# Causal attention on one core: the weights of three query blocks turned by VectorE and carried through DRAM

## The chip, the cores and the metric

The program runs on one core of one Trainium2 chip. A core has five engines that work side by side and wait for each other by semaphores: TensorE (PE in the rows; its weight loads, which overlap its products, are PEld), VectorE (DVE), ScalarE (ACT), GpSimd (POOL) and SyncE (SP), which here issues nearly all DMAs. TensorE writes into PSUM, and VectorE or ScalarE must move a result from there to SBUF before TensorE can read it. The metric is the device time of one execution in microseconds (us); lower is better.

## The reference

Three layers in a row. The first is banded attention (8 heads), the second a channel mix with three large products. The third, the one that the change touches, is causal attention by four experts with a gate that keeps two of them per token:

```python
# x: 4 batches, 576 tokens, 512 features; E = 4 experts, Hd = 64
logits = x @ w_gate                      # the 2 best experts of a token, softmax over their logits
for e in range(E):
    q, k, v = x @ wq[e], x @ wk[e], x @ wv[e]
    scores = q @ k.transpose(0, 2, 1) / 8
    scores = np.where(np.triu(np.ones((S, S)), 1), -1e9, scores)   # causal
    a = softmax(scores)                  # (…, 576, 576), zero above the diagonal
    out += gate_weight(e) * (a @ v @ wo[e])
```

The weights `a` come out with queries on the partitions and keys along the row. The product with `v` sums over keys, and TensorE sums over partitions, so each 128x128 block of `a` on or below the diagonal has to be turned first.

## The kernel before

Everything is float32; most products run as three products of a high and a low part (F32R), the turning and `a @ v` as plain float32.

The first two layers fill the program up to about 391 us. Neither their code nor the order of their instructions changes. Then comes the third layer, batch by batch (b = 0 to 3) and expert by expert (e = 0 to 3). The 576 tokens are cut into five blocks `TB`: one of 64 and four of 128. Its steps are generators:

- `queries_keys(b, g)` makes queries and keys for the expert pair g (experts 2g and 2g+1): 48 products of 288 columns (`pq`, `pk`, L394), a split into high and low parts, and 12 DMAs on SP (L681) that lay the parts out as `qs`, `kk` and `kl2`.
- `values(b)` makes `v` and the gate: 60 products of 260 columns (`pv`, L694).
- `scores(b, e)`: per query block t two products per piece of the row (`sc`, L768 and L770), a masked minimum on DVE into the row buffer `pe` (L774), the exponential with its row sum on ACT (L780); when all five blocks are there, three small DVE steps (L784 to L787), and then the scaling of the weights by 1/sum and gate, blocks 0 to 3 on DVE (L795) and block 4 on ACT (L793).
- `context(b, e)`: the 15 blocks are turned on PE as a product with `ident` (L815), four per PSUM tile, and copied to SBUF by ACT (L820) and DVE (L822) as `wt`. After the odd expert of a pair the products with `v` follow, key block by key block, for both experts at once on the two halves of TensorE's columns: widths of 512, 64, 512, 384, 256 and 128 columns (`av`, L841 and L846). Each float32 product leaves two records in the trace. Two copies give `ctx`.
- `project(b)`: 30 products of 512 columns with `wo` (`po`, L868) and 5 stores.

Which steps run beside which is set by a table `plan`: for each (b, e) it lists the generators and how many pieces of each `merge` takes in turn. From the program that results, a scheduler makes the order on each engine with cost estimates of its own; on the chip each engine then works its list off in that order. The same holds for SP: a DMA whose source is not ready holds up all DMAs behind it.

The buffers that matter: two row buffers `pe`, ten `wt` tiles, and PSUM tiles for scores (2), turned blocks (2), the `av` sum (1) and the other products (3).

Of the kernel before, what the change touches and what calls it, by code (L numbers as in the profile page):

```python
# [16 lines left out]
NEG = -8.0e9  # L17
# [4 lines left out]
def tile_dilated_attention__rwkv_channel_mix__moe_attention(  # L22
# [31 lines left out]
    xpool = ctx.enter_context(tc.tile_pool(name="xpool", bufs=1, side="left"))  # L54
    psum = dict(zip(("sc", "pt", "av", "mm"), [2, 2, 1, 3]))
    psum["pool"] = ctx.enter_context(tc.tile_pool(name="psum", bufs=2, space=bass.MemoryType.PSUM))

# [8 lines left out]
    still = cpool.tile([128, 512], BF16, name="still")  # L66
# [11 lines left out]
    def band(name, base, p1=0, j1=0):  # L78


        m = cpool.tile([128, WK], F32, name=name)
# [413 lines left out]
    with tc.tile_pool(name="apool", bufs=2, side="left") as ap:  # L495
# [90 lines left out]
        run(ga)  # L586

# [4 lines left out]

    TB = [(0, 64), (64, 128), (192, 128), (320, 128), (448, 128)]
    NB = len(TB)
    PO = [0, 64, 256, 576, 1024, 1600]
    NC2 = 3 * E * HD + E

    with s2:
        w2p = s2.enter_context(tc.tile_pool(name="w2p", bufs=1, side="left", reuse_waits="tile"))
        ep1 = s2.enter_context(tc.tile_pool(name="ep1", bufs=2, side="left", reuse_waits="tile"))  # L600
        def split_y(b):
            y = X[b][:, :, 1 : S + 1]
            yh = ep1.tile([128, KT, S], F32R, tag="yh", name=f"yh_{b}", bufs=1)
            yl = ep1.tile([128, KT, S], F32R, tag="yl", name=f"yl_{b}", bufs=1)
            for kt in range(KT):
                nc.scalar.copy(yh[:, kt, :], y[:, kt, :])
                nc.gpsimd.tensor_sub(yl[:, kt, :], y[:, kt, :], yh[:, kt, :].bitcast(F32))  # L607
            return yh, yl
# [4 lines left out]
        cmask = w2p.tile([128, S], F32, name="cmask")  # L613
        nc.gpsimd.memset(cmask, 0.0)
        nc.gpsimd.affine_select(out=cmask, in_=cmask, pattern=[[-1, S]], base=448,
                                channel_multiplier=1, compare_op=ALU.is_ge, fill=NEG)
# [3 lines left out]
        ahead = split_y(0)  # L620
        rawo = [w2p.tile([128, DM], F32, name=f"w2oraw{g}") for g in range(2)]
# [9 lines left out]
        for g in range(2):  # L631
            nc.sync.dma_start(rawo[g], wo[2 * g : 2 * g + 2].rearrange("e d f -> (e d) f"))
# [4 lines left out]
        for g in range(2):  # L637
            nc.scalar.copy(woh[:, g, :], rawo[g])
            nc.vector.tensor_sub(wol[:, g, :], rawo[g], woh[:, g, :].bitcast(F32))
# [5 lines left out]
        def begin(b, parts):  # L645


            qs = [ep.tile([128, 2, S], F32R, tag=f"qs{g}", name=f"qs_{b}_{g}", bufs=1) for g in range(2)]
# [4 lines left out]
            done[b] = (qs, kk, kl2, vt, gt)  # L653
            ys[b] = parts

        def queries_keys(b, g):

            qs, kk, kl2, vt, gt = done[b]
            yh, yl = ys[b]
# [4 lines left out]
            for c in range(2):  # L664
                cs = slice(CH * c, CH * c + CH)
                pq = ps("mm", f"pq_{b}_{g}_{c}")[:, :CH]
                pk = ps("mm", f"pk_{b}_{g}_{c}")[:, :CH]
                product(pq, (w2h, w2l), (yh[:, :, cs], yl[:, :, cs]), range(KT),
                        slice(128 * g, 128 * g + 128))
                product(pk, (w2h, w2l), (yh[:, :, cs], yl[:, :, cs]), range(KT),  # L670
# [5 lines left out]
                if c == 1:  # L676
                    emitted.add(("k", b, g))
                    for dst, src in ((qs[g][0:64], qh), (kk[g][0:64], kh), (qs[g][64:128], ql), (kk[g][64:128], kh),
                                     (kl2[g][0:64], kl), (kl2[g][64:128], kl)):
                        for j in range(2):  # L680
                            nc.sync.dma_start(dst[:, j, :].bitcast(F32), src[64 * j : 64 * j + 64, :].bitcast(F32))  # L681
                yield

        def values(b):

            qs, kk, kl2, vt, gt = done[b]
            yh, yl = ys[b]
            lg = logits[b % 2]
            for t, (t0, tn) in enumerate(TB):
                p = ps("mm", f"pv_{b}_{t}")[:tn, :260]  # L690
# [34 lines left out]
        def place(kb, t):  # L725

            t0 = TB[t][0]
            if kb == 0:
                return (3, 256) if t == 0 else (0, t0 - 64)
            if kb == 1:  # L730
                return 1, t0 - 64
            if kb == 2:
                return 2, t0 - 192
            if kb == 3:
                return 3, t0 - 320
            return 2, 384

        groups = [[(0, t) for t in range(1, NB)], [(1, t) for t in range(1, NB)],
                  [(2, 2), (2, 3), (2, 4), (4, 4)], [(3, 3), (3, 4), (0, 0)]]
        regions = [[(64, 0, 512)], [(128, 0, 512)], [(128, 0, 512)], [(128, 0, 256), (64, 256, 320)]]  # L740

# [5 lines left out]
        done, ys = {}, {}  # L747
# [4 lines left out]
        def scores(b, e):  # L752

            qs, kk, kl2, vt, gt = done[b]
# [3 lines left out]
            pe = ep1.tile([128, PO[NB]], F32, tag="pe2", name=f"pe2_{nm}", bufs=2)  # L758
            st = stats[e % 2]
            for t, (t0, tn) in enumerate(TB):  # L760
                n = t0 + tn
                tn = 128
                parts = [(0, n)] if n <= 512 else [(64, n), (0, 64)]
                for i, (c0, c1) in enumerate(parts):
# [3 lines left out]
                    nc.tensor.matmul(sc, qs[g][:, e % 2, t0 : t0 + 128], kk[g][:, e % 2, c0:c1],  # L768
                                     start=True, stop=False)
                    nc.tensor.matmul(sc, qs[g][:, e % 2, t0 : t0 + 128], kl2[g][:, e % 2, c0:c1],  # L770
                                     start=False, stop=True)
                    m = cmask[:tn, 448:512] if t == 0 else cmask[:, S - n + c0 : S - n + c1]
# [26 lines left out]
        heads = {}  # L799

        def context(b, e):

            vt = done[b][3]
            pe = weights.pop((b, e))
            g = e // 2
            nm = f"{b}_{e}"
            heads[e % 2] = []
            moved = []
            for i, grp in enumerate(groups):
                pt = ps("pt", f"pt2_{nm}_{i}")  # L810
                for kb, t in grp:
                    k0, kn = TB[kb]
                    tn = 128
                    c0 = place(kb, t)[1]
                    nc.tensor.transpose(pt[:kn, c0 : c0 + tn], pe[:tn, PO[t] + k0 : PO[t] + k0 + kn], ident[:tn, :tn])  # L815
                wt = ep.tile([128, 512], F32, tag="wt", name=f"wt{i}_{nm}", bufs=10)
                heads[e % 2].append(wt)
                for rows, c0, c1 in regions[i]:
                    if ("aava", "avav")[e % 2][i] == "a":
                        moved.append(nc.scalar.copy(wt[:rows, c0:c1], pt[:rows, c0:c1]))  # L820
                    else:
                        moved.append(nc.vector.tensor_copy(wt[:rows, c0:c1], pt[:rows, c0:c1]))  # L822
                yield
            if e % 2 == 0:
                return
            av1 = ps("av", f"av1_{nm}")
            av0 = ps("pt", f"av0_{nm}")
            two = [(64 * x, heads[x], vt[:, :, 64 * (2 * g + x) : 64 * (2 * g + x) + 64]) for x in range(2)]

            def after_all(ins):  # L830

                if kb == 0:
                    for m in moved:
                        tc.add_manual_dep(ins.ins, m.ins.name, together, reason="both experts' products together")

            for kb in range(NB):
                k0, kn = TB[kb]
                i, c0 = place(kb, max(kb, 1))
                q0 = max(k0, 64)
                for p0, w, vh in two:  # L840
                    ins = nc.tensor.matmul(av1[p0 : p0 + 64, q0 - 64 : 512], vh[:kn, kb, :], w[i][:kn, c0 : c0 + S - q0],  # L841
                                           start=(kb == 0), stop=(kb == NB - 1))
                    after_all(ins)
                if kb == 0:
# [13 lines left out]
        def project(b):  # L858

            for t, (t0, tn) in enumerate(TB):  # L860
# [9 lines left out]
                ob = ep.tile([128, DM], F32, tag="ob", name=f"ob_{b}_{t}", bufs=5)  # L870
# [7 lines left out]
        begin(0, ahead)  # L878
# [5 lines left out]
        def late(b):  # L884
            begin(b, split_y(b))
# [11 lines left out]
        plan = {(0, 0): [("c", 4), ("l1", 1), ("k0", 2), ("s", 6)],  # L897
# [55 lines left out]
```

## Time and profile before

| | us |
|---|---|
| median of three runs (597.89 to 602.9) | 601.97 |
| span of the profiled execution, first to last instruction | 600.2 |
| PE busy in the span | 568.9 |
| DVE busy | 334.7 |
| ACT busy | 369.2 |

A busy time is the time in which at least one instruction of the engine was under way. For the profiled execution only the span is known; it lies 1.8 us under the median of the runs and 2.3 us over the fastest of them. The third layer takes the last 209 us of the span.

### The profile page before, as it was taken

Reading aid. Unit: us, or ns where it says so; the run is one execution under the profiler, and the core shown is the slowest. Engines: PE = TensorE matmul, PEld = TensorE weight load, DVE = VectorE, ACT = ScalarE, POOL = GpSimd, SP = SyncE. Lnnn points to the kernel's source line nnn. Section 1 sums busy time; section 2 is a strip of 40 time slices with the busy share of each in tenths; the row PEclk is TensorE's granted clock in tenths of the full one; section 3 lists DMA queues with packets and bytes.
Section 4 is the critical chain, followed back from the end, with each engine's and each line's share of the span. In section 5 each row is a group of like instructions: output and inputs, shape, how many; then the busy total and the mean of one; then the engine's idle time right before and its main releaser. Section 6 shows DMA issues by size and latency. Waiting matters only on the chain.

```text
span 600.2 us, 12777 instructions
## 1 busy us (share of the span) xinstructions
PE 568.9 (95%) x4749; PEld 505.4 (84%) x4752; DVE 334.7 (56%) x1112; ACT 369.2 (62%) x1004; POOL 79.5 (13%) x101
## 2 busy tenths in 40 slices
PE   8987896999999999999999999999998999999986
PEld 4657796888999999999999999999986988987753
DVE  3567988854655355347254253527566556656552
ACT  3789957655698266597364742327656756755751
POOL 8300000000323012130003313003003003000000
PEclk9987889899999999999999999999999999999997
DMA  9990276638431321210000140043604514505302
GB/s 172 171 331 28 70 195 136 117 76 139 81 63 25 70 44 28 37 25 21 1 1 1 31 112 1 2 106 94 156 5 115 142 57 119 122 25 137 115 1 79
DMA packets 120461, 48.81 MB, mean 81 GB/s; under 512 B 104320, under 2 KB 108496, under 8 KB 120400
## 3 DMA queue, kind: packets, MB, share of 16 engines
q1 hardware_dynamic: 119984, 47.57, 34.4%
q8 instruction: 37, 0.61, 0.4%
q0 software_dynamic: 416, 0.44, 0.4%
q14 instruction: 24, 0.20, 0.1%
HBM read 29.11 MB, written 4.72 MB: 56 GB/s over the span
## 4 chain that ended last, share of the span: by engine, by line
PE 74%; ACT 13%; DVE 7%; issue 2%; DMA 2%; POOL 1%; SPq 0%; DVEq 0%; POOLq 0%; ACTq 0%
PE v L394 17%; PE h L394 13%; PE pv L694 5%; PE av L841 5%; PE pt L815 4%; PE po L868 4%; PE sc L267 4%; PE pk L394 4%; PE z L394 4%; PE pq L394 4%; PE av L304 3%; PE pt L294 2%; ACT pe L280 2%; PE sc L770 2%; PE sc L768 2%
## 5 line engine op out<-in xcount | busy, mean ns | idle before, releaser
L394 PE MATMUL h<-xh,wk_hi 128*128 128x288 f32 x256 | 80.2, 314 | 6.5 <-ACT r L407 4.2
L394 PE MATMUL h<-xl,wk_hi 128*128 128x288 f32 x256 | 77.8, 304 | 0.6 <-DVE xl L373 0.6
L394 PE MATMUL h<-xh,wk_lo 128*128 128x288 f32 x256 | 77.1, 301 | 0.0
L394 PE MATMUL v<-kh,wv_hi 128*128 128x288 f32 x256 | 76.2, 302 | 0.0
L394 PE MATMUL v<-kl,wv_hi 128*128 128x288 f32 x256 | 75.8, 299 | 0.0
L394 PE MATMUL v<-kh,wv_lo 128*128 128x288 f32 x256 | 75.0, 296 | 0.0
L394 PEld LDWEIGHTS h<-xh,wk_hi 128*128 128x128 f32 x256 | 49.5, 194 | 9.8 <-ACT r L407 5.3
L384 POOL TENSOR_TENSOR xl<-m,xh 128x1152 fp32r<-128x1152 f32 x12 | 32.1, 2674 | 168.5 <-ACT xh L383 148.9
L780 ACT ACTIVATE pe<-pe,st 128x64 f32<-128x64 f32 (+4 forms) x80 | 44.9, 563 | 15.3 <-DVE st L774 15.2
L394 PEld LDWEIGHTS h<-xl,wk_hi 128*128 128x128 f32 x256 | 49.5, 193 | 1.2 <-DVE xl L373 0.9
L394 PEld LDWEIGHTS h<-xh,wk_lo 128*128 128x128 f32 x256 | 49.6, 194 | 0.1
L394 PEld LDWEIGHTS v<-kh,wv_hi 128*128 128x128 f32 x256 | 47.8, 188 | 0.9 <-DVE r L408 0.2
L394 PEld LDWEIGHTS v<-kl,wv_hi 128*128 128x128 f32 x256 | 48.0, 188 | 0.5
L394 PEld LDWEIGHTS v<-kh,wv_lo 128*128 128x128 f32 x256 | 48.0, 188 | 0.2
L774 DVE CUSTOM_DVE_ANT_0 pe<-sc,cmask 128x64 f32<-128x64 f32 (+4 forms) x80 | 37.0, 475 | 19.5 <-PE sc L770 18.3
L280 ACT ACTIVATE pe<-pe,st 128x96 f32<-128x96 f32 x108 | 39.4, 368 | 13.2 <-DVE st L276 12.9
L407 ACT ACTIVATE r<-h 128x288 f32<-128x288 f32 x64 | 25.5, 409 | 30.4 <-PE h L394 21.6
L394 PE MATMUL z<-xh,wr_hi 128*128 128x288 f32 x128 | 39.9, 313 | 2.5 <-ACT z L401 2.5
L417 DVE TENSOR_TENSOR x<-v,z 128x288 f32<-128x288 f32 x32 | 14.5, 455 | 46.8 <-PE v L394 46.7
L370 DVE SCALAR_TENSOR_TENSOR m<-x,mus,m 128x288 f32<-128x288 f32 x64 | 30.0, 513 | 18.9 <-ACT m L369 18.7
L607 POOL TENSOR_TENSOR yl<-x,yh 128x576 fp32r<-128x576 f32 x16 | 20.8, 1332 | 138.4 <-DVE sm L713 46.4
L394 PE MATMUL z<-xh,wr_lo 128*128 128x288 f32 x128 | 39.1, 306 | 0.0
(169 smaller groups left out, 1522.4 us busy)
## 6 DMA issues: line engine op xcount, KB each, us to landing
kk<-kh SPq DMA_DIRECT2D x32, 144.0 KB, 2.6
kl<-kl SPq DMA_DIRECT2D x32, 144.0 KB, 2.6
raw_in_moe_w_k_dram<-in_moe_w_k_dram SPq DMA_DIRECT2D x4, 1024.0 KB, 9.5
raw_in_moe_w_v_dram<-in_moe_w_v_dram SPq DMA_DIRECT2D x4, 1024.0 KB, 5.7
out_dram<-ob SPq DMA_DIRECT2D x16, 256.0 KB, 2.5
rqk<-in_q_dram SPq DMA_DIRECT2D x48, 72.0 KB, 2.5
rqk<-in_k_dram SPq DMA_DIRECT2D x48, 72.0 KB, 2.5
vw<-in_v_dram SPq DMA_DIRECT2D x16, 192.0 KB, 3.5
```

The source lines that it names most:

```text
L267: nc.tensor.matmul(sc[h, c0 : c0 + WK], qT[h, QB * t : QB * t + QB], kT[h, k0 : k0 + WK], start=(b > 0), stop=(b > 0 or t == t1 - 1))
L280: nc.scalar.activation(pe[:, t, :], pe[:, t, :] if b else sc[:, c0 : c0 + WK], AF.Exp, bias=st[:, 0, t : t + 1], scale=-1.0, accum_out=st[ ...
L370: nc.vector.scalar_tensor_tensor(out=m, in0=x, scalar=mus[:, 0, w, f : f + 1], in1=m, op0=ALU.mult, op1=ALU.add)
L384: nc.gpsimd.tensor_sub(lo, m, hi.bitcast(F32))
L394: nc.tensor.matmul(o, w[:, kt, wsl], x[:, kt, :], start=(n == 0), stop=(n == last))
L407: nc.scalar.activation(r, p, AF.Relu)
L694: nc.tensor.matmul(p, x[:, kt, t0 : t0 + tn], w[:, kt, 512:772], start=(n == 0), stop=(n == 3 * KT - 1))
L774: nc.vector.tensor_tensor_reduce(out=pe[:tn, PO[t] + c0 : PO[t] + c1], in0=sc, in1=m, scale=-0.125, scalar=(BIG if i == 0 else st[:tn, 1, ...
L780: nc.scalar.activation(pb, pb, AF.Exp, bias=st[:tn, 0, t : t + 1], scale=-1.0, accum_out=st[:tn, 2, t : t + 1])
L815: nc.tensor.transpose(pt[:kn, c0 : c0 + tn], pe[:tn, PO[t] + k0 : PO[t] + k0 + kn], ident[:tn, :tn])
L841: ins = nc.tensor.matmul(av1[p0 : p0 + 64, q0 - 64 : 512], vh[:kn, kb, :], w[i][:kn, c0 : c0 + S - q0], start=(kb == 0), stop=(kb == NB - 1))
L868: nc.tensor.matmul(p, x[:, t0 : t0 + tn], w[:, g, :], start=(n == 0), stop=(n == 5))
```

## The change

It does five things, all in the third layer.

1. **Tokens padded.** 64 zero tokens are put ahead of the 576 (`PAD`), so that all five query blocks have 128 rows and the weight rows fall into 15 slots of 128 columns (`SLOT`: block t has t + 1 of them). The row buffers become two fixed tiles `pes`, `qs` and `yh`, `yl` become fixed tiles as well; GpSimd writes the zeros once.
2. **Turning.** For the first 14 experts the 12 slots of query blocks 2 to 4 are turned by one VectorE instruction, 32x32 block by 32x32 block (L814 of the changed kernel), into `tp`. That puts each 32x32 block right but leaves the blocks themselves in the wrong quarter of the partitions. One DMA stores `tp` in DRAM (L816, 768 KB), and four DMAs read it back into `wt` (L818, 192 KB each, to 32 partitions each) with the quarters exchanged. The 3 slots of blocks 0 and 1 stay on PE with one copy. For the last two experts all 15 slots stay on PE.
3. **Products by query block.** The products with `v` go over query blocks t and, for each, over key blocks up to t: per expert 14 products of 128 columns and one of 64 (L843), where there were five of 512 to 128 and one of 64. `context` now stands by itself after the odd expert.
4. **Plan.** One plan for all batches, with `context` after it; `project(b-1)` moves to the same place in each batch.
5. **Small moves.** `wo` is loaded and split later, once the memory of the second layer is free (before, it was loaded ahead); the causal mask is made later; the last three output tiles use a free `wt` buffer.

```diff
+    PAD = 64
     TB = [(0, 64), (64, 128), (192, 128), (320, 128), (448, 128)]
-    PO = [0, 64, 256, 576, 1024, 1600]
+    SLOT = [0, 1, 3, 6, 10, 15]
+    FAR = 2
+    NEAR = {FAR: [(0, 3)], NB: [(0, 3), (3, 6), (6, 10), (10, 13), (13, 15)]}
+    PO = [128 * s + PAD for s in SLOT]
...
+        pes = [ep.tile([128, 128 * SLOT[NB]], F32, name=f"pe2_{i}", bufs=1) for i in range(2)]
...
+        def split_wo():
+            for g in range(2):
+                raw = ep.tile([128, DM], F32, tag="ob", name=f"w2oraw{g}", bufs=3)
+                nc.sync.dma_start(raw, wo[2 * g : 2 * g + 2].rearrange("e d f -> (e d) f"))
+                nc.scalar.copy(woh[:, g, :], raw)
+                nc.vector.tensor_sub(wol[:, g, :], raw, woh[:, g, :].bitcast(F32))
...
-        def context(b, e):
...
+        def turn(b, e):
             pe = weights.pop((b, e))
...
+            wt = ep.tile([128, 4, SLOT[NB], 32], F32, tag="wt", name=f"wt_{nm}", bufs=3)
+            far = FAR if (b, e) < (B - 1, 2) else NB
+            if far < NB:
+                n = SLOT[NB] - SLOT[far]
+                tp = ep.tile([128, 4, n, 32], F32, tag="tp", name=f"tp_{nm}", bufs=1)
+                nc.vector.transpose(tp, pe[:, 128 * SLOT[far] :].rearrange("p (s g a) -> p g s a", g=4, a=32))
+                moved = dram.tile([128, 4, 32 * n], F32, tag="m", name=f"moved_{nm}", bufs=2)
+                nc.sync.dma_start(moved, tp.rearrange("p g s b -> p g (s b)"))
+                for g in range(4):
+                    nc.sync.dma_start(wt[32 * g : 32 * g + 32, :, SLOT[far] :, :].rearrange("a i s b -> a i (s b)"),
+                                      moved[:, g, :].rearrange("(i a) x -> a i x", i=4))
+            yield
+            for n, (s0, s1) in enumerate(NEAR[far]):
+                pt = ps("pt", f"pt2_{nm}_{n}")
+                for sl in range(s0, s1):
+                    nc.tensor.transpose(pt[:, 128 * (sl - s0) : 128 * (sl - s0) + 128], pe[:, 128 * sl : 128 * sl + 128], ident)
...
+        def context(b, g):
...
+            for t in range(NB):
+                for kb in range(t + 1):
                     for p0, w, vh in two:
-                        after_all(nc.tensor.matmul(av0[p0 : p0 + 64, 0:64], vh[:64, 0, :], w[3][:64, 256:320],
-                                                   start=True, stop=True))
+                        o = av1[p0 : p0 + 64, 128 * t - 128 : 128 * t] if t else av0[p0 : p0 + 64, 0:64]
+                        nc.tensor.matmul(o, vh[:, kb, :], w[:, 0 if t else 2 : 4, SLOT[t] + kb, :],
+                                         start=(kb == 0), stop=(kb == t))
...
-        plan = {(0, 0): [("c", 4), ("l1", 1), ("k0", 2), ("s", 6)],
...
+        plan = {0: [("t", 6), ("s", 6), ("k", 2)],
+                1: [("t", 6), ("s", 6), ("l", 1), ("q", 2)],
+                2: [("t", 6), ("s", 6), ("p", 5)],
+                3: [("t", 6), ("v", 6), ("s", 6)]}
...
+                if e % 2:
+                    run(context(b, e // 2))
```

How the order moves at three places. In the names `pt2_1_1` is batch 1, expert 1; `av1_1_1` of the kernel before names the odd expert of the pair, that of the changed kernel the pair.

On PE before, batch 1, the products of the first pair, four key blocks and the short first query block, stand in one piece:

```order
L841 MATMUL av1_1_1_5884<-wt0_1_0_5698,vt_1_5148 64x512
L841 MATMUL av1_1_1_5884<-wt0_1_1_5840,vt_1_5148 64x512
L846 MATMUL av0_1_1_5885<-wt3_1_0_5824,vt_1_5148 64x64
L846 MATMUL av0_1_1_5885<-wt3_1_1_5876,vt_1_5148 64x64
L841 MATMUL av1_1_1_5884<-wt1_1_0_5750,vt_1_5148 64x512
L841 MATMUL av1_1_1_5884<-wt1_1_1_5853,vt_1_5148 64x512
```

On PE now, the same pair, where the products that need slots read back from DRAM begin:

```order
L398 MATMUL pq_2_1_0_6294<-yh_4591,w2l_4596 128x288
L398 MATMUL pq_2_1_0_6294<-yh_4591,w2h_4595 128x288
L398 MATMUL pq_2_1_0_6294<-yl_4592,w2h_4595 128x288
L843 MATMUL av1_1_0_5954<-wt_1_1_5813,vt_1_5283 64x128
L843 MATMUL av1_1_0_5954<-wt_1_0_5686,vt_1_5283 64x128
```

They stand amid the queries of the next batch; 21 more of 128 columns follow at once, by turns from the odd and the even expert's `wt`. Between the last score product of expert 1 and this place PE now has 15 `po`, 60 `pv`, 8 `pq`, 22 score products of experts 2 and 3, 6 turnings and 7 products of 128 or 64 columns that need only the slots turned on PE or the even expert's.

On DVE before, a piece of the same stretch with the copies of expert 1's turned blocks:

```order
L673 TENSOR_TENSOR ql_2_1_6130<-pq_2_1_0_6134,qh_2_1_6132 128x288
L822 COPY wt3_1_1_5876<-pt2_1_1_3_5872 128x256
L822 COPY wt3_1_1_5876<-pt2_1_1_3_5872 64x64
L774 ISA pe2_1_2_5842,st20_4900<-sc2_1_2_4_0_5898,cmask_4587 128x512
L774 ISA st20_4900 128x1
```

On DVE now, the turning of expert 1, right behind its scaling but for one minimum of the next expert:

```order
L797 TENSOR_SCALAR pe2_1_4903<-pe2_1_4903,st21_4917 128x320
L797 TENSOR_SCALAR pe2_1_4903<-pe2_1_4903,st21_4917 128x448
L776 ISA pe2_0_4902,st20_4916<-sc2_1_2_2_0_5885,cmask_4893 128x320
L776 ISA st20_4916 128x1
L814 STREAM_TRANSPOSE tp_1_1_5814<-pe2_1_4903 128x1536
```

One long instruction has taken the place of the copies. On SP before, the end of the layout DMAs of batch 2, first pair:

```order
L681 DMA kk_2_0_5945<-kh_2_0_5962 64x576 x2
L681 DMA kl2_2_0_5947<-kl_2_0_5964 64x576 x4
L875 DMA out_0_dram<-ob_0_3_6093 128x512
L875 DMA out_0_dram<-ob_0_4_6119 128x512
L681 DMA qs_2_1_5944<-qh_2_1_6132 64x576 x2
```

On SP now, the same layout DMAs:

```order
L700 DMA kk_2_0_5827<-kh_2_0_5842 64x576 x2
L816 DMA moved_1_1_5816<-tp_1_1_5814 128x1536
L700 DMA kl2_2_0_5829<-kl_2_0_5844 64x576 x4
L877 DMA out_0_dram<-ob_0_1_6032 128x512
L818 DMA wt_1_1_5813<-moved_1_1_5816 32x4x384 x4
L877 DMA out_0_dram<-ob_0_2_6047 128x512
```

The store and the four loads of expert 1 have come in between, and the loads wait in SP's list until the store has landed.

## Rows read from the trace of the kernel before

**Rows 1.** The page, busy us by engine (share of the span) xinstructions.

```profile
PE 568.9 (95%) x4749; PEld 505.4 (84%) x4752; DVE 334.7 (56%) x1112; ACT 369.2 (62%) x1004; POOL 79.5 (13%) x101
```

**Rows 2.** Busy time by stretch: us, engines (xcount), granted clock, DMA share, GB/s.

```profile
400.00:575.00 175.00, 171.84 (x1227) 148.41 (x1226) 106.44 (x449) 113.71 (x306) 15.44 (x12) 1.00 0.39 100
575.00:601.00 26.00, 17.34 (x80) 10.26 (x78) 7.92 (x22) 6.68 (x16) 0.00 (x0) 0.79 0.13 46
448.80:458.50 9.70, 7.88 (x51) 6.43 (x49) 8.71 (x30) 8.68 (x22) 5.14 (x4) 1.00 0.76 182
```

**Rows 3.** Groups by line: busy us, mean ns | idle before, releaser.

```profile
L815 PE MATMUL pt<-ident,pe 128*128 128x128 f32 (+1 forms) x240 | 35.6, 278 | 3.6 <-DVE pe L795 2.3 <-DVE wt L822 0.8 <-ACT wt L820 0.5
L841 PE MATMUL av<-wt,vt 64*64 64x512 f32 (+4 forms) x160 | 29.7, 501 | 1.2 <-DVE wt L822 1.1
L822 DVE COPY wt<-pt 128x512 f32<-128x512 f32 (+2 forms) x32 | 15.4, 502 | 13.8 <-PE pt L815 13.4
```

**Rows 4.** The chain that ended last, in order of time: start, us, what.

```profile
498.53 1.58 PE pk L394 x12
...
506.66 1.01 PE av L841 x4
507.67 0.11 PE av L846 x4
507.78 2.30 PE av L841 x16
...
511.32 0.87 PE pt L815 x8
...
518.11 1.38 PE po L868 x6
...
527.92 1.87 PE pv L694 x15
```

**Rows 5.** The same view in the first layer: float32 products of 64 columns.

```profile
205.29 0.73 PE av L304 x20
```

**Rows 6.** Groups by line and form: VectorE's turning in the first layer.

```profile
L241 DVE STREAM_TRANSPOSE kT<-rqk 128x576 f32<-128x576 f32 x6 | 7.2, 1205 | 0.2 <-DMA rqk<-in_k_dram 0.2
L246 DVE STREAM_TRANSPOSE kT<-rqk 128x576 f32<-128x576 f32 x6 | 4.6, 770 | 2.9 <-DMA rqk<-in_k_dram 2.9
```

**Rows 7.** Timeline, batch 2, from an odd expert's last score product to its scaled weights.

```profile
516.41 0.28 PE L770 MATMUL sc<-kl,qs 128*128 128x64 f32 x1
...
517.08 0.28 DVE L774 CUSTOM_DVE_ANT_0 pe<-sc,cmask,st 128x64 f32<-128x64 f32 x1
...
518.94 1.14 DVE L795 TENSOR_SCALAR pe<-pe,st 128x64 f32<-128x64 f32 x4
```

**Rows 8.** DMA issues: count, KB each, median us from issue to landing.

```profile
raw_in_moe_w_v_dram<-in_moe_w_v_dram SPq DMA_DIRECT2D x4, 1024.0 KB, 5.7
out_dram<-ob SPq DMA_DIRECT2D x16, 256.0 KB, 2.5
vw<-in_v_dram SPq DMA_DIRECT2D x16, 192.0 KB, 3.5
w2oraw<-in_moe_wo_dram SPq DMA_DIRECT2D x2, 256.0 KB, 3.9
```

**Rows 9.** Timeline of SP: four layout DMAs issued one after the other.

```profile
521.82 2.47 SPq L681 DMA_DIRECT2D kl<-kl  x4
```

**Rows 10.** Busy time of a stretch full of layout DMAs (64 partitions each).

```profile
504.00:508.80 4.80, 4.80 (x35) 3.34 (x35) 3.39 (x16) 3.09 (x9) 2.36 (x2) 1.00 0.78 190
```

**Rows 11.** Waits after 400 us: who for whom, us in total, times, longest.

```profile
PE av L841 <- DVE wt L822: 1.1, 2, 0.7
PE pt L815 <- DVE wt L822: 0.8, 1, 0.8
PE pt L815 <- ACT wt L820: 0.5, 1, 0.5
```

**Rows 12.** Timeline of PE after the last scores: the first wait.

```profile
581.67 1.19 PE L815 MATMUL pt<-ident,pe 128*64 128x128 f32 x8 [1.18 <-DVE pe L795]
```

**Rows 13.** The end of the chain that ended last: the last pair's products.

```profile
585.74 1.97 PE av L841 x4
...
587.92 3.48 PE av L841 x16
```

More of the change, by code (lines that the diff above doesn't have):

```diff
@@ L54, in tile_dilated_attention__rwkv_channel_mix__moe_attention @@
     xpool = ctx.enter_context(tc.tile_pool(name="xpool", bufs=1, side="left"))
+    sm = ExitStack()
+    mpool = sm.enter_context(tc.tile_pool(name="mpool", bufs=1, side="left"))
     psum = dict(zip(("sc", "pt", "av", "mm"), [2, 2, 1, 3]))
     psum["pool"] = ctx.enter_context(tc.tile_pool(name="psum", bufs=2, space=bass.MemoryType.PSUM))
+    dram = ctx.enter_context(tc.tile_pool(name="dram", bufs=2, space=bass.MemoryType.DRAM))
     def ps(tag, name):
@@ L586, in tile_dilated_attention__rwkv_channel_mix__moe_attention @@
         run(ga)
+    sm.close()
     run(gd, 24)
@@ L619, in tile_dilated_attention__rwkv_channel_mix__moe_attention @@
         raw = [ep1.tile([128, 2, NC2], F32, tag="pe2", name=f"w2raw{i}", bufs=2) for i in range(2)]
-        ahead = split_y(0)
-        rawo = [w2p.tile([128, DM], F32, name=f"w2oraw{g}") for g in range(2)]
+        split_y(0)
         for i in range(2):
@@ L723, in values @@
             yield
[L725 to L740, printed above, removed]
         logits = [ep.tile([128, NB, E], F32, name=f"lg{i}", bufs=1) for i in range(2)]
@@ L797, in scores @@
             yield
-        heads = {}
-        def context(b, e):
-            vt = done[b][3]
+        turned = {}
+        def turn(b, e):
             pe = weights.pop((b, e))
-            g = e // 2
             nm = f"{b}_{e}"
[L807 to L822, printed above, removed]
-                yield
[L824 to L844, printed above, removed]
@@ L845, in context @@
+        def context(b, g):
+            vt = done[b][2]
+            av1 = ps("av", f"av1_{b}_{g}")
+            av0 = ps("pt", f"av0_{b}_{g}")
+            two = [(64 * x, turned.pop((b, 2 * g + x)), vt[:, :, 64 * (2 * g + x) : 64 * (2 * g + x) + 64]) for x in range(2)]
+            for t in range(NB):
+                for kb in range(t + 1):
                     for p0, w, vh in two:
-                        after_all(nc.tensor.matmul(av0[p0 : p0 + 64, 0:64], vh[:64, 0, :], w[3][:64, 256:320],
-                                                   start=True, stop=True))
+                        o = av1[p0 : p0 + 64, 128 * t - 128 : 128 * t] if t else av0[p0 : p0 + 64, 0:64]
+                        nc.tensor.matmul(o, vh[:, kb, :], w[:, 0 if t else 2 : 4, SLOT[t] + kb, :],
+                                         start=(kb == 0), stop=(kb == t))
@@ L869, in project @@
                         n += 1
-                ob = ep.tile([128, DM], F32, tag="ob", name=f"ob_{b}_{t}", bufs=5)
+                if last and t > 2:
+                    if t == 3:
+                        spare = ep.tile([128, 4, SLOT[NB], 32], F32, tag="wt", name="spare", bufs=3).rearrange("p i s b -> p (i s b)")
+                    ob = spare[:, 512 * (t - 3) : 512 * (t - 2)]
+                else:
+                    ob = ep.tile([128, DM], F32, tag="ob", name=f"ob_{b}_{t}", bufs=3)
                 if last and t % 2 == 0:
@@ L876, in project @@
                 yield
-        begin(0, ahead)
+        begin(0)
         run(queries_keys(0, 0))
@@ L884, in late @@
         def late(b):
-            begin(b, split_y(b))
+            begin(b)
+            split_y(b)
+            if b == 1:
+                split_wo()
             yield
@@ L918, in tile_dilated_attention__rwkv_channel_mix__moe_attention @@
                     gens["s"] = scores(b1, e1)
-                merge(*[(part(gens[k], n), n) for k, n in plan[(b, e)]])
-        for b in range(B):
-            run(gens[f"p{b}"])
+                else:
+                    gens.pop("s")
+                if b + 1 == B:
+                    plan = {0: [("t", 6), ("s", 6), ("k", 2)], 1: [("t", 6), ("s", 6), ("p", 5)],
+                            2: [("t", 6), ("s", 6)], 3: [("t", 6)]}
+                of = {"k": f"k{b}", "l": f"l{b + 1}", "q": f"q{b + 1}", "v": f"v{b + 1}", "p": f"p{b - 1}"}
+                merge(*[(part(gens[k], n), n) for k, n in [(of.get(k, k), n) for k, n in plan[e]] if k in gens])
+                if e % 2:
+                    run(context(b, e // 2))
+        run(gens[f"p{B - 1}"])
 _INS = ['q', 'k', 'v', 'moe_mu_k', 'moe_mu_r', 'moe_w_k', 'moe_w_v', 'moe_w_r',
```

76 lines of the change are left out of this document (41 added, 35 removed), and 15 rows, old and new, of the table plan.

## The prediction, made before the changed kernel ran

> **What bounds the kernel now.** I read the page first: PE is busy 95% of the span, no other engine over 62% [rows 1]. Then the stretches of the third layer, since only that layer changes: from 400 to 575 us PE idles 3.2 of 175 us at the full clock, DVE is busy 61% [rows 2]. So up to 575 us the time is PE's work, and a change pays by PE work that it takes away and costs by waits that it gives PE. The last 26 us are another regime: PE is busy 17.3 of them at a mean granted clock of 0.79 [rows 2].
>
> **What the change takes from PE.** The groups by line show 240 turnings (L815), 35.6 us of busy time [rows 3]; since products overlap, the price on PE's path is read from the chain: 8 in 0.87 us, 0.109 each [rows 4]. 14 experts lose 12 of their 15 turnings: 168 x 0.109 = **-18.3 us**.
>
> **The products with v.** Before, a pair takes 1.01 + 0.11 + 2.30 = 3.42 us [rows 4]. Now it has 14 groups of 128 columns and one of 64, each with four records (two experts, two records each): as many columns, but 60 records instead of 24. Narrow groups of this kind are in the first layer, 64 columns: 20 records in 0.73 us, so 0.146 a group [rows 5]. A line through 64 columns at 0.146 and 512 at 1.01 gives 0.27 for 128, and 14 x 0.27 + 0.146 = 3.92, 0.5 more than before. The other bound is by columns alone: 1280 columns in 2.30 us [rows 4] make 0.23 for 128, 14 x 0.23 + 0.115 = 3.3, 0.1 less. I take 0.3 more, times eight pairs: **+2.4** (-0.8 to +4.0).
>
> **Turning on VectorE.** The trace has 576-column turnings on DVE at 770 ns where both sides are read in rows, at 1205 ns where single elements are scattered [rows 6]. The new one has runs of 32 elements on both sides, nearer to the first: 1536 columns at 1.34 ns are 2.05 us (3.2 at the dearer). 14 of them are 28.7 us of DVE; 14 copies of 384 columns remain, half on DVE, about 0.56 each, 3.9 us; of the 15.4 us of copies on DVE [rows 3] nearly all go. DVE thus rises from 106 [rows 2] to about 124 us in a stretch that shrinks to some 160: 77%. DVE works off its list in order, so scores behind a 2 us turning wait, and with two PSUM tiles for scores PE waits after them. What that does is seen from 448.8 to 458.5 us: DVE is busy 8.71 of 9.7 us, PE only 7.88 [rows 2], so 1.8 us are lost where DVE is at 90%. I put two such stretches, less a little: **+3** (0 to +13; 13 is 8% of the stretch).
>
> **The detour through DRAM** is the wait that decides. The products with v need the loaded slots of the odd expert. How long after its last score product are they there? Scaled weights: from 516.69 (516.41 + 0.28) to 520.08 (518.94 + 1.14), 3.4 us [rows 7]. On DVE one minimum stands before the turning, 0.5, then 2.05. The store is 768 KB: 256 KB out take 2.5 us, 1024 KB in take 5.7 [rows 8], between them by size 4.6. The loads stand behind the store's landing in SP's list; four issues are 0.62 us apart [rows 9], and 192 KB land in 3.5 us [rows 8], so the last lands after 3 x 0.62 + 3.5 = 5.4. With 0.15 for the two hand-overs to SP (an estimate) that makes **16.1 us**. The ends: 12.4 with a store as quick as 256 KB and loads of 2.5 us, 19.9 with the dear turning, a store of 5.7, half a microsecond of waiting in SP's list and loads at the pace of the layout DMAs, 190 GB/s [rows 10], 4.1 us for 786 thousand bytes plus 2.5 of landing. I take 16.1, since the rows used are those nearest in size.
>
> Against it stands the PE work that the new order puts between. For the pair shown there are 15 `po` (0.23 each: 6 in 1.38), 60 `pv` (0.125), 8 `pq` (0.13, like `pk`: 12 in 1.58) [rows 4], 22 score products of 64 to 512 columns (0.23 at 512 like `po`, less below; 0.17 on average, an estimate), 6 turnings and 7 narrow products: 3.4 + 7.5 + 1.1 + 3.8 + 0.7 + 0.5 = 17.0. Counted in the same way the seven pairs that use the detour have some 16.8, 16.0, 17.0, 15.1, 16.5, 14.7 and 10.8 us. In the last there is little other work, and two experts' scores there are paced by DVE and ACT, so I take 12.3 of real time. PE then waits 0, 0.1, 0, 1.0, 0, 1.4 and 3.8 us: **+6.5** with rounding (+1.7 if the chain is 14 us, +31 at 19.9).
>
> The layout DMAs, 64 partitions each, move 190 GB/s at a DMA share of 0.78 [rows 10]. A rule of the Trainium skill explains that and speaks against this transfer (SBUF — State Buffer, "Door 1: The DMA port swizzle"): a DMA to 32 or 64 partitions reaches 8 of the 16 ports, 189 GB/s measured at 1 MiB, and two DMAs to disjoint halves serialize. By the page the four loads move for 786 / 189 = 4.2 us (an estimate) where a load over all partitions would need 2.4 at its 328 GB/s; the time that comes of it is the second rival's, from rows.
>
> **Smaller terms.** PE waits for copies of turned blocks 1.1 + 0.8 + 0.5 us [rows 11], of which about half lies in the end stretch; **-1.2** (0 to -2.4). `wo`, loaded late, stands ahead of the first layout DMAs on SP and of key copies on ACT; its landing takes 3.9 us [rows 8] from the moment that the second layer's memory is free (about 391.5), and the copies behind it come about 1 us late: **+0.5** (0 to 1). The longer tokens cost no columns: the first block's products already moved 260 columns with 64 rows of weights. GpSimd's zeros and mask, 14 short instructions, lie under the first 48 `pq` and `pk` and 60 `pv`, 48 x 0.13 + 60 x 0.125 = 13.7 us; without that cover they would delay the first scores by their own length. The layout DMAs now wait behind stores and loads on SP, up to 5 us; in the order shown a whole expert's scores lie between their issue and their use. The end: before, PE waits 1.18 us for the last scaled weights [rows 12] and 1.2 more for copies, and then the last pair runs at the low clock, 1.97 + 3.48 [rows 13] instead of 1.01 + 2.30 us. Now the other pair's products and 15 turnings fill those waits: **-2** (-4 to +3; the + if PE idles before them and the clock falls earlier).
>
> **Sum.** -18.3 + 2.4 + 3 + 6.5 - 1.2 + 0.5 - 2 = -9.1 us. The profiled span goes from 600.2 to 591.1; the median of the runs, 1.8 above it, from 602.0 to **593**.
>
> **Rivals.**
> - *The detour hides wholly.* Chain of 14 us or less and no loss to DVE: waits +1.7, DVE 0, so -16.9: 585. For it: the store may be as quick as the 256 KB one, whose rows are the only stores. Against: the loads alone need 4 us.
> - *The loads run at the pace of the layout DMAs.* 6.6 instead of 5.4 us, chain 17.3, waits 0.5, 1.3, 0.3, 2.2, 0.8, 2.6 and 5.0 = 12.7 instead of 6.5: 599. For it: same queue, half the partitions.
> - *VectorE sets the pace.* 77% busy in long pieces; PE loses 8% of 160 us, 13 instead of 3, while the waits for loads shrink to 4 because they run in parallel: 600 to 601. For it the stretch at 448.8 us, against it that DVE has 23% left.
> - *Slower: the loads land after the products' turn, pair after pair.* From a chain of some 17.7 us on, the waits sum to over 15 us and eat the gain; each further microsecond costs seven. At 19.9: +15, 617. For it: every step of the chain is taken from smaller or other transfers, and SP must come to the loads at once. Against: it needs several dear ends together.
>
> **How the numbers follow.** Chances: forecast 0.38 (587 to 598), hidden wholly 0.17 (581 to 587), loads at the slow pace 0.15 (596 to 603), VectorE 0.12 (597 to 606), slower 0.18 (606 to 622). Within 1% of 602, about what a measurement of this kernel can tell from no change, is 596 to 608. Faster: 0.33 + 0.17 + 0.06 = 0.56; same: 0.05 + 0.12 + 0.09 + 0.01 = 0.27; slower the rest, 0.17. The range of 8 in 10 is 583 to 608: it leaves out the slower case nearly whole and the best end of the hidden one.
>
> **What would show it.** In the changed profile: turnings on PE 72 instead of 240; DVE's turning of 1536 columns near 2 us; the store landing near 4.6 and a load near 3.5 us; PE's idle time before L843, released by the loads, about 6 us in all and most before the last pair that uses them; PE's idle time before scores released by DVE about 3 us more. If a pair's products take over 4 us without waiting, the record price is wrong; if PE waits more than 2 us before most pairs, the chain is; if PE idles all over the stretch without a DMA as releaser, VectorE is the bound. The forecast is most easily wrong in the landing times, where 1 us is worth 7.

## The result, and the profile after

| | us | ratio to before, 95% interval |
|---|---|---|
| before, median of 8 runs | 598.83 | |
| changed, median of 8 runs (603.09 to 608.09) | 605.71 | 1.0085 (1.0057 to 1.0113) |
| span of the changed kernel's profiled execution | 603.8 | |

The forecast was 593, a gain of 9.1 us on the 602 of the first three runs of the kernel before; by eight runs that kernel takes 598.83. The changed kernel is 0.9% slower than it. The page, as [rows 1]:

```profile
PE 563.0 (93%) x4869; PEld 505.7 (84%) x4872; DVE 346.7 (57%) x1106; ACT 353.8 (59%) x968; POOL 82.9 (14%) x115
```

168 turnings are gone, but PE's busy time fell by only 5.9 us, and its share fell too: PE works longer on something else, and it waits. Busy time by stretch, as [rows 2]; columns: stretch, us, PE, PEld, DVE, ACT, POOL busy (xcount), granted clock, DMA share, GB/s:

```profile
400.00:575.00 175.00, 161.46 (x1260) 143.22 (x1258) 116.28 (x432) 96.33 (x266) 15.48 (x12) 0.98 0.82 220
575.00:603.80 28.80, 23.16 (x173) 17.23 (x172) 11.01 (x33) 8.95 (x21) 0.00 (x0) 0.86 0.28 83
467.20:470.60 3.40, 2.72 (x26) 2.72 (x28) 0.00 (x0) 0.00 (x0) 0.00 (x0) 0.50 0.58 239
573.00:583.20 10.20, 9.67 (x32) 6.65 (x33) 6.48 (x29) 6.49 (x17) 0.00 (x0) 0.50 0.65 200
```

PE idles 13.5 us up to 575 where it idled 3.2, the DMA share is 0.82 where it was 0.39, and twice PE runs at the lower level, 1.2 in place of 2.4 GHz: for 3.4 us from 467.2 and for 10.2 us from 573.0. Groups by line, as [rows 3, 6] (busy us, mean ns | idle before, releaser), and under them PE's waits, as [rows 11] (us in total, times, longest):

```profile
L843 PE MATMUL av<-wt,vt 128*64 128x128 f32 (+1 forms) x480 | 37.3, 282 | 11.3 <-DMA wt<-moved 8.8 <-issue 1.2 <-DVE wt L830 1.1
L814 DVE STREAM_TRANSPOSE tp<-pe 128x1536 f32<-128x1536 f32 x14 | 24.8, 1775 | 0.7 <-ACT pe L795 0.7
L824 PE MATMUL pt<-ident,pe 128*128 128x128 f32 x72 | 14.9, 312 | 0.2
```

```profile
PE av L843 <- DMA wt<-moved: 8.8, 5, 3.4
PE av L843 <- issue: 1.2, 1, 1.2
PE av L843 <- DVE wt L830: 1.1, 1, 1.1
PE pv L713 <- ACT ob L876: 1.1, 1, 1.1
PE sc L772 <- DMA kl<-kl: 0.8, 1, 0.8
```

The loads are the largest wait, but 8.8 us of waits against 18 us of turnings saved leaves a gain. A large part of the rest is in the products. The timeline of PE in two places (start, us, what), then the same products in one piece:

```profile
422.29 0.43 PE L843 MATMUL av<-wt,vt 128*64 128x128 f32 x2 [1.14 <-DVE wt L830]
422.65 0.40 PE L398 MATMUL pk<-yh,w2h 128*128 128x288 f32 x1
422.89 0.29 PE L398 MATMUL pk<-yl,w2h 128*128 128x288 f32 x1
...
454.28 0.27 PE L824 MATMUL pt<-ident,pe 128*128 128x128 f32 x1
454.48 0.33 PE L843 MATMUL av<-wt,vt 128*64 128x64 f32 x2
454.74 0.44 PE L824 MATMUL pt<-ident,pe 128*128 128x128 f32 x2
...
443.83 2.83 PE L843 MATMUL av<-wt,vt 128*64 128x128 f32 x46 [1.24 <-DMA wt<-moved]
```

In the piece of 46 records the next instruction starts 2.77 us after the first: 0.06 us a record. The single product of 64 columns at 454.48 stands alone between other work: the next instruction starts 0.26 us later, though its two records are worth 0.06 in a piece (0.11 for four [rows 4]). The one of 128 columns at 422.29 takes 0.36 where 0.12 is usual. The product that follows comes late as well: the key product at 422.65 takes 0.24 where those behind it take 0.13 to 0.14. A turning has the same effect (0.22 for a query or key product right behind one, in the kernel before too), so part of a piece's price is that of the change from one kind of product to another. Before, the products of a pair stood in one piece, 8 pieces in all; now PE meets them in 33.

DMA issues, as [rows 8]: median us from issue to landing.

```profile
moved<-tp SPq DMA_DIRECT2D x14, 768.0 KB, 5.5
wt<-moved SPq DMA_DIRECT2D x56, 192.0 KB, 4.0
out_dram<-ob SPq DMA_DIRECT2D x14, 256.0 KB, 4.4
```

The output rows that landed in 2.5 us before [rows 8] now take 4.4.

So that the runs can be compared, PE's time from the first query product to its last record is split: each record gets the time from the end of the record before it (or its own start, if later) to its own end; what is left is idle; of the time of a record at the lower clock half is taken out and listed as lost.

| us | layer starts | pieces | turnings | products with v | other four kinds | idle | lost to the clock | sum |
|---|---|---|---|---|---|---|---|---|
| before | 391.6 | 8 | 27.6 | 27.5 | 139.4 | 6.0 | 3.0 | 203.6 |
| changed | 392.5 | 33 | 9.6 | 34.0 | 142.3 | 14.1 | 6.2 | 206.2 |
| e1_together | 390.3 | 8 | 9.6 | 26.8 | 140.4 | 25.8 | 9.3 | 211.9 |
| e2_all_pe | 390.1 | 8 | 28.2 | 26.7 | 137.9 | 0.9 | 0 | 193.7 |
| e3_free | 389.6 | 14 | 9.6 | 28.0 | 142.7 | 11.2 | 1.6 | 193.1 |
| e5_scatter | 390.4 | 38 | 29.0 | 33.4 | 142.1 | 2.1 | 0 | 206.5 |
| e6_dve_only | 390.6 | 8 | 30.3 | 26.8 | 138.0 | 4.7 | 0 | 199.7 |
| e8_even | 392.8 | 8 | 19.4 | 26.7 | 138.9 | 7.4 | 1.7 | 194.0 |
| e9_even_ob | 392.3 | 8 | 19.3 | 26.7 | 138.8 | 3.4 | 0 | 188.2 |
| e10_dma2 | 390.2 | 8 | 28.6 | 26.7 | 138.7 | 11.5 | 3.4 | 208.9 |
| e12_before_free | 393.1 | 32 | 27.9 | 45.9 | 142.3 | 2.0 | 0 | 218.1 |

The first two layers are alike in all of them, and the layer starts between 389.6 and 393.1; the 0.9 us by which it starts later in the changed kernel lie inside that spread.

### The profile page after: what moved, and what is told of

The parts are those of the page before. It is cut to its first block, busy times and chain, and to the rows that moved or that the text cites. A ratio compares the mean times of both kernels' runs of the same rounds, so it can differ in the third digit from the quotient of the medians.

```text
span 603.8 us, 13122 instructions
## 1 busy us (share of the span) xinstructions
PE 563.0 (93%) x4869; PEld 505.7 (84%) x4872; DVE 346.7 (57%) x1106; ACT 353.8 (59%) x968; POOL 82.9 (14%) x115
## 5 line engine op out<-in xcount | busy, mean ns | idle before, releaser
L843 PE MATMUL av<-wt,vt 128*64 128x128 f32 (+1 forms) x480 | 37.3, 282 | 11.3 <-DMA wt<-moved 8.8
L843 PEld LDWEIGHTS av<-wt,vt 128*64 128x64 f32 x480 | 29.7, 142 | 19.4 <-issue 11.3
```

The lines of the kernel that those rows point to most:

```text
L843: nc.tensor.matmul(o, vh[:, kb, :], w[:, 0 if t else 2 : 4, SLOT[t] + kb, :], start=(kb == 0), stop=(kb == t))
```

## The experiments

Each ran beside the kernel before, whose median was 599.3 to 601.4. Median us and ratio stand with each.

**The products in one piece, and the detour undone.** Four of the runs are two by two: products free or in one piece, detour or all turnings on PE.

```diff
# e1_together: the rule of the kernel before, put back for every query block
-                        nc.tensor.matmul(o, vh[:, kb, :], ...)
+                        ins = nc.tensor.matmul(o, vh[:, kb, :], ...)
+                        if kb == 0:
+                            for m in moved_by[(b, 2 * g)] + moved_by[(b, 2 * g + 1)]:   # copies and loads
+                                tc.add_manual_dep(ins.ins, m.ins.name, together, ...)
# e5_scatter: no detour, nothing else;  e2_all_pe: both edits
-            far = FAR if (b, e) < (B - 1, 2) else NB
+            far = NB
```

> The changed kernel, but the 30 products of a pair may start only when all slots of both experts are there, so that they stand in one piece: 8 pieces in place of 33. In the changed kernel a record of the products costs 0.07 us inside a piece, but PE loses about 0.28 us for each piece (on entering it and on leaving it). Theory A, the broken-up products are a main loss: products and the work right behind them fall by 25 x 0.28 = 7 us; the 7 groups that no longer run ahead of the loads make the waits for loads longer by 1 to 1.5 us in some five pairs, 10 to about 16 us; together 601 to 606. Theory B, narrow products cost more wherever they stand (60 records in place of 24): products on PE's path stay near 34 us, waits grow as under A, 609 to 613. Theory C, only the waits for loads count: like B.

> As the run before it in this list (products of a pair in one piece), but all 15 slots of all experts are turned on PE: no turning on VectorE, no store, no loads. Padding, plan and products by query block stay as in the changed kernel. Theory A (detour and broken-up products are what costs): no wait for a DMA, no fall of the clock but at the end, 168 x 0.107 = 18 us of turnings come back: 598 to 601, as the kernel before. Rival D, plan or padding themselves cost 3 us or more: 603 to 608, with idle time on PE that no DMA ends.

> The changed kernel with all 15 slots of all experts turned on PE and nothing else altered: the detour alone is undone, the products of a pair are free to start as their slots come (38 pieces by the order, against 8 in the all-PE run before). Theory A: 30 pieces more at 0.28 us each, 8 us over the all-PE run with whole products (591.4): 598 to 601. Rival: pieces cost only where PE waits for loads anyway: 591 to 593.

| | detour | all turnings on PE |
|---|---|---|
| products free | 605.71, 1.0085 (changed) | 604.33, 1.0081 (1.0051 to 1.0111) |
| products in one piece | 608.26, 1.0140 (1.0105 to 1.0174) | 591.43, 0.9860 (0.9831 to 0.9888) |

Undoing the detour alone changes nothing that can be measured; undoing it in the kernel with whole products takes off 17 us. e1: products fell from 34.0 to 26.8 us, 7.2 where theory A said 7 and theory B none; the others fell by 1.9. The time rose all the same, to 2 us above A's range, since idle time rose from 14.1 to 25.8 and the clock took 3.1 more. Of the idle time 7.9 us came up right before the products: the 7 narrow groups, some 1.3 us a pair, had been work under the wait for the loads. e2 came out 7 us under A's range and 1.4% under the kernel before. e5 ran 3 us over its range: 30 pieces more cost 12.9 us, 0.43 each; by the table 6.7 of them lie in the products, 5.0 in the other work and 1.2 in idle time. In e2 a pair looks like this on PE's timeline:

```profile
502.99 3.39 PE L845 MATMUL av<-wt,vt 128*64 128x64 f32 x60
```

The next instruction starts 3.33 us after it, where a pair took 3.42 before [rows 4]: 60 records cost no more than 24 when they stand together. PE's waits after 391 us in e2, all of them of 0.1 us or more in total:

```profile
PE av L845 <- ACT wt L830: 0.5, 1, 0.5
PE pt L826 <- DVE wt L832: 0.3, 2, 0.2
```

**The same rule taken from the kernel before.**

```diff
             def after_all(ins):
-                if kb == 0:
-                    for m in moved:
-                        tc.add_manual_dep(ins.ins, m.ins.name, together, ...)
+                return
```

> The kernel before, with nothing changed but that the products of a pair may start as soon as their own blocks are turned (the rule that held both experts' products together is left out, as in the changed kernel): 32 pieces in place of 8 by the order. If a piece costs 0.36 us, the mean that the products and their neighbours lost per extra piece in the changed kernel, 24 more cost 8.6 us; the wait of 1.1 us for the last copies may go: 606 to 609 against 600. Rival, pieces cost PE only with products of 128 columns: 598 to 601.

617.72 us, 1.0277 (1.0234 to 1.0321): 16 us for 24 pieces, twice what was expected and far from the rival. The reason is on the timeline of this run:

```profile
426.29 1.07 PE L839 MATMUL av<-wt,vt 64*64 64x512 f32 x2
427.29 0.33 PE L694 MATMUL pv<-w2h,yh 128*64 128x260 f32 x1
```

A product of 512 columns of one expert alone (2 records) takes 1.00 us; with the other expert's on the other half of the columns (4 records) it took 1.01 [rows 4]. In these runs the two halves work side by side only when both products follow each other at once. A piece that holds one expert alone gives that up, and the wider the product, the dearer: by the table the products take 18.4 us more than before.

**What the loads, VectorE and the traffic cost.**

```diff
# e3_free: far products read a constant tile, loads run on unread
-  w[:, 0 if t else 2 : 4, SLOT[t] + kb, :]
+  (fixed[:, :, kb, :] if t >= FAR and (b, 2 * g) < (B - 1, 2) else w[:, 0 if t else 2 : 4, SLOT[t] + kb, :])
# e6_dve_only: e2, and before the turnings on PE
+                nc.vector.transpose(tp, ...)          # tp is not read
# e7_dma_only: e2, and
+                nc.vector.tensor_copy(tps[:, 0, 0, 0:1], pe[:, 384:385])      # the trigger
+                nc.sync.dma_start(moved, tps...)
+                for g in range(4):
+                    nc.sync.dma_start(tps[32 * g : 32 * g + 32]..., moved[:, g, :]...)
# e10_dma2: e2, and
+                nc.sync.dma_start(moved..., pe[:, 384:])
+                for g in range(4):
+                    nc.sync.dma_start(junk[32 * g : 32 * g + 32]..., moved[:, g, :]...)
```

> The first run of this list, but the far products of the first 14 experts read a constant tile in place of the slots that come back from DRAM, so nothing waits for the loads (the output is not the reference's); turning, store and loads all still run. The order has 14 pieces of products. Theory A: without the waits for loads and without the fall of the clock behind the longest of them, 12 to 18 us under the first run, 586 to 591: what the change would be worth with its latency hidden. Rival E, the traffic or VectorE's long turnings cost PE by themselves: over 595, with idle time on PE behind VectorE or ScalarE.

> The all-PE run with whole products (591.4), and in addition the 14 turnings on VectorE into a tile that nobody reads; no store, no loads. In the run in which nothing waited for the loads PE saved 18.6 us of turnings against the all-PE run and the time came out the same. Theory V, VectorE's list: a 1.8 us turning holds up minima, splits and copies behind it, and PE waits: 14 x 0.7 to 1.2 = 10 to 16 us more, 600 to 607. Theory T, the traffic did it: within 2 us of 591.4.

> The all-PE run with whole products (591.4), and in addition the store and the four loads of 14 experts from and to a tile that nobody needs; no turning on VectorE but one element as a trigger. Theory T, the traffic (layout DMAs and outputs wait behind it on SP and share the DMA engines): 599 to 606, with PE idle behind layout DMAs or output buffers. Theory V: within 3 us of 591.4.

> The run with only the traffic again, without its flaw (there VectorE's trigger waited 46 us for the loads of the expert before): all 15 slots on PE; for 14 experts a store of 768 KB straight from the scaled weights and four loads into a tile that nobody reads. Against 591.4 of the all-PE run. Theory T: PE idles behind layout DMAs and output tiles, 597 to 602. Theory V (VectorE's turnings, 6 us by their own run, are the larger part): 592 to 595.

e3: 592.42, 0.9869 (0.9847 to 0.9892), between A and E: 15.8 us less than e1, yet no less than e2, which turns everything on PE. PE idles 11.2 us in it, longest behind VectorE's scaling and ACT's output copies:

```profile
PE pt L829 <- DVE pe L800: 3.2, 2, 2.5
PE pv L716 <- ACT ob L884: 2.6, 2, 1.9
```

So in this form the detour for all earns nothing even with its latency hidden. e6: 597.45, 0.9971 (0.9951 to 0.9991): VectorE's list costs 6.0 us, under V's 10 and over T's 2. e7: 619.01, 1.0321 (1.0286 to 1.0356), says nothing on its question, since the trigger made VectorE wait for the loads of the expert before (VectorE's waits, this run):

```profile
DVE tps L819 <- DMA tps<-moved: 46.3, 13, 5.2
```

e10, without that: 606.92, 1.0139 (1.0103 to 1.0174), 15.5 us more than e2 and above T's range. ACT's and VectorE's waits in e10 show through what:

```profile
ACT ob L881 <- DMA out_dram<-ob: 13.7, 4, 4.1
```

```profile
DVE kl L694 <- DMA kl<-kl: 7.6, 3, 4.6
```

Output tiles and key tiles come free only when their DMAs land; these stand behind the stores and loads in SP's list and share the DMA engines. What PE waits for in e10:

```profile
PE pv L713 <- ACT ob L881: 4.3, 2, 3.3
PE pt L826 <- ACT wt L830: 3.1, 1, 3.1
PE pt L826 <- DVE wt L832: 1.9, 3, 1.5
PE po L870 <- DVE kl L694: 1.1, 2, 0.9
```

The clock takes 3.4 more. That e10 stores from the row buffers themselves does not explain it: the trace shows no engine waiting for a row buffer that a store still reads. How the two costs add up is not shown: 6.0 and 15.5 make 21.5, and e3, which saves 18.6 us of turnings against e2 and is 1.0 slower, pays 19.6; but by the table 6.1 of that are no waits, they lie in the products and the other work (14 pieces in place of 8, and another order).

**Loads in another shape.** The four loads by quarters of the row in place of quarters of the partitions:

```diff
# e4_wide
-  wt[32 * g : 32 * g + 32, :, far:, :]  <-  moved[:, g, :].rearrange("(i a) x -> a i x", i=4)
+  wt[:, i, far:, :]                     <-  moved[32 * i : 32 * i + 32].rearrange("a g x -> g a x")
# e11_wide2: moved is [4, 4, 32, x], stored in four DMAs of 32 partitions
+  wt[:, i, far:, :]                     <-  moved[i].rearrange("g a x -> (g a) x")
```

> The first run of this list, but each of the four loads goes to all 128 partitions (a quarter of the row) in place of 32 partitions with whole rows: same number of DMAs, same bytes, same 1536-byte pieces. Rule of the ports (a DMA to 32 partitions reaches half of them): from the first load's issue to the last landing 4 to 4.8 us in place of 6, PE's waits for loads 6 to 9 us less than in the first run. Rival F, issue distance and fixed latency set the landing: within 0.5 us of 6, the time within 2 us of the first run.

> The run with whole products and the detour for all, with loads to 128 partitions again, but with 128 rows outermost in source and target (in the first try the outermost count was 4, and some 4 DMA engines worked at a time); for that the store is made in four DMAs from 32 partitions each. Rule of the ports with rows spread: first load's issue to last landing 4 to 5 us in place of 5.7, store as long as before or 1 us longer by its issues: time 602 to 608, against 608.3. Rival: number of packets and issue distance set it, loads 5.5 us and the store 1 to 2 us longer: 610 to 616.

e4: 677.01, 1.1275 (1.1250 to 1.1299), 69 us over e1 where 6 to 9 less were expected. Stretches in which loads run, of e4 and then of the changed kernel:

```profile
644.00:647.00 3.00, 0.00 (x0) 0.00 (x0) 0.00 (x0) 0.00 (x0) 0.00 (x0) 0.50 0.27 97
```

```profile
496.00:499.00 3.00, 3.00 (x23) 2.62 (x21) 3.00 (x9) 1.59 (x4) 0.00 (x0) 1.00 1.05 236
```

With an outermost count of 4 in the loads' source the share of 16 DMA engines is 0.27, about four of them, at 97 GB/s; with 32 it is full at 236. e11 has 128 outermost: a load lands 3.2 us after its issue (median; 4.0 in e1), store and loads together take 9.2 us in place of 10.7. But each load waits there for its own quarter of the store alone, so that the loads begin while the store is still under way, and their issues are spread over 2.7 us in place of 1.35. From the first load's issue to the last landing it is 6.1 us, 6.2 in e1, where 4 to 5 were expected. And its time, 611.69, 1.0211 (1.0172 to 1.0251), lies in the rival's range and not under e1's: before products PE waits 19 us in both, and the clock takes 13.5 in place of 9.3. The Trainium skill's rule on ports (SBUF — State Buffer, "Door 1: The DMA port swizzle") is not shown by this: the shorter landing of one load can as well come from fewer loads at a time. That transfers to disjoint halves serialize (same page, "Can I just issue two DMAs to hit both halves?") is not borne out here: for one of 32 partitions that page gives 189 GB/s, and four of them, two on each half, moved 236 together. Whether PE would gain from loads over all partitions stays open.

**The detour where there is time for it.** The even expert of a pair has the odd one's scores between its turning and its use:

```diff
# e8_even, on top of e1_together
+            far = FAR if (b, e) < (B - 1, 2) and e % 2 == 0 else NB
# e9_even_ob: the same, output tiles ob
-                    ob = ep.tile([128, DM], F32, tag="ob", ..., bufs=3)
+                    ob = ep.tile([128, DM], F32, tag="ob", ..., bufs=5)
```

> Whole products as in the all-PE run, but the even experts of the pairs (7 of them, without the last pair) take the detour, the odd ones are turned on PE. The even expert's slots have the whole odd expert's scores more to come back, over 10 us, so no wait for loads. PE saves 7 x 12 x 0.107 = 9 us against 591.4. If detours cost what they cost in the run without load waits (about 17 us for 14), 8.5 us go again: 589 to 592. Rival: those costs come only when two detours follow each other closely: 583 to 586.

> The run with the detour for even experts only, with five output tiles in place of three. There PE lost 4.0 us before products with the v weights, behind ACT's copies of output rows, which wait for an output tile whose store stands behind loads in SP's list, and 1.7 us to the clock that fell after the longer of these waits. If the tiles are the cause: 4 to 6 us less than 593.5, so 587.5 to 589.5, and less than the all-PE run (591.4). Rival: ACT then waits at the next thing that the loads hold up on SP: 592 to 594.

e8: 593.46, 0.9893 (0.9861 to 0.9924), 1.5 us over the upper end of what was expected and far from the rival: no wait of PE for a load is left, but the output tiles cost as in e10. PE's waits in e8:

```profile
PE pv L713 <- ACT ob L881: 4.0, 2, 2.7
PE pk L398 <- DVE ql L692: 1.6, 1, 1.6
PE sc L770 <- DVE st L776: 0.6, 1, 0.6
```

e9: 587.56, 0.9795 (0.9768 to 0.9821), inside the expected range. The first of these rows is gone, the other two are the same, and the clock stays at its upper level. This is the fastest version: 2.0% under the kernel before, and 0.7% under e2, each by its ratio to before. e2 with five output tiles was not run; it had only 0.9 us of idle time to lose.

## Why the prediction was wrong

The layer's sum in the table rose by 2.6 us where the forecast's terms make -9.1. Of the nearly 12 us between them 0.3 lie in the turnings, 4.1 in the products, 2.9 in the work around them, and 4.5 in idle time and clock together (11.3, where the other terms make 6.8). Term by term:

- **Turnings, -18.3.** Right: 27.6 to 9.6 us, -18.0.
- **Products, +2.4.** This is the step that failed. I costed 14 groups of 128 columns as if they stood together, and chose 3.7 us for a pair between bounds of 3.3 and 3.9. Together they take 3.33, at the bound by columns. But the diff also takes away the rule that held both experts' products together (`after_all`, in the diff shown), and I gave that no price; I even counted the 7 narrow products as cover for the loads. Measured +6.5 us in the products and +2.9 in what stands around them. e1, e5 and e12 show the cause: put back, -7.2 and -1.9 in these two; left out elsewhere, +12.9 and +16 us of time.
- **The detour, +6.5.** The waits for loads, with the one put down to issue, are 10.0; all idle time rose by 8.1. The chain from the last score product to the last landing is 18.4 us (median of the seven odd experts) where I had 16.1: the store takes 5.5 in place of 4.6, the loads 6.0 in place of 5.4, and store issues wait up to 2 us on SP. The rows were of DMAs that ran with fewer others. The bounds held it. (Their lower end, 12.4 us, comes to 13.0 with the terms named there; nothing hangs on it.)
- **The end, -2.** The waits went as forecast: after 575 us PE idles 0.5 us where it idled 2.8. The clock went the other way, as the upper bound allowed, 6.2 us lost in place of 3.0: the longest wait for loads (3.4 us) and three waits of 0.8 to 1.9 before 573 precede the two falls. e2 shows what the change gives without detour and pieces: nothing lost to the clock and 0.9 us idle in the layer where there were 6.0. This, not the detour, is the good part of the change; plan, padding and small moves were not taken apart.
- **VectorE, +3.** The turning takes 1.775 us, not 2.05, and PE waits 0.2 us before scores for VectorE where the forecast had 3 (0.4 more before `po`, 1.1 for a copy of turned blocks); alone the turnings cost 6.0 (e6).
- **Copies, -1.2, and `wo`, +0.5.** PE waits 1.1 us for copies of turned blocks, in place of 2.4 [rows 11]: as forecast. The layer starts 0.9 us later, which the spread of the starts does not tell from nothing.
- **Not in the sum.** What the traffic does to the tiles of others. It decides e10 and e8; in the changed kernel PE waits 1.1 us behind output copies and 0.8 for `kl`, and the rest may lie under longer waits.

The rival on late loads had a right mechanism with too high a price: from a chain of 17.7 us on it put the waits at over 15 us, and with 18.4 they are 10.0. That 605.7 lies within the stated range of 583 to 608, and at the upper edge of the VectorE rival's, is luck: both were made for waits, and the largest miss is in the products. Against e5 the account of the detour is even: 19.4 us of turnings saved, 12.0 more idle, 6.2 more lost to the clock, 0.8 in the rest.

## What to carry to other kernels

A line that a diff takes away can be a rule of order, and needs a price like any instruction; where two products share TensorE's columns by halves, the price is that of losing the partner and of changing from one kind of product to another. Here a transfer in place of TensorE work paid only where its consumer was far away (e9), and only once the tiles whose DMAs stand behind it in the queue were counted too. Undo the parts of a change two by two: here one part (-8.5 us) and another (+13) hid each other, and the named part, for all experts, was worth nothing.

## What the runs showed of the hardware

- Plain float32 products of 64 columns of TensorE's width on either half overlap fully when one follows the other at once: 1.00 us for one of 512 columns alone, 1.01 for two.
- A small product of that kind between others costs 0.26 us (64 columns) or 0.36 (128), in a piece its two records take about 0.06 or 0.12.
- A DMA whose source has an outermost count of 4 kept a share of 0.27 of the DMA engines, 97 GB/s, against 1.05 and 236 with 32; the bytes and the 1536-byte pieces were the same.
- VectorE turns 1536 columns of float32 in 1.775 us, 1.16 ns a column, less than for 576 columns [rows 6].
